# An elementwise product moved from VectorE to GpSimd, and two exponentials set apart, in a fused attention and MLP kernel

## The chip, the cores and the metric

The kernel runs on one core of a Trainium2 chip. The time is the device time of one execution in microseconds (us); before the change it is 575.52 us, the median of three runs (574.96 to 576.21). A core has five engines with a queue of instructions each, worked off in order: TensorE (PE, matrix products), VectorE (DVE), ScalarE (ACT), GpSimd (POOL) and SyncE (SP, which here issues transfers). They wait for one another through semaphores. SBUF is the working memory with 128 partitions, PSUM the memory into which TensorE writes.

## What is computed

```python
def rmsnorm(x, g):
    rms = np.sqrt(np.mean(x * x, axis=-1, keepdims=True) + 1e-06)
    return x / rms * g
# q, k, v: batch 8, 12 heads, 448 positions, 64 per head
q_n, k_n = rmsnorm(q, g_q), rmsnorm(k, g_k)
scores = q_n @ k_n.T / sqrt(64)
attn = softmax(scores) @ v                 # [8, 12, 448, 64]
x = attn.transpose(0, 2, 1, 3).reshape(8, 448, 768)
h = (x.T @ U @ V).T                        # mixing over positions, rank 32
u = x + h
out = u + relu(u @ w_ch1) @ w_ch2          # 768 -> 3072 -> 768
```

(The reference, shortened; inputs and output are float32.)

## The kernel before

The kernel works on two heads at a time. Such a pair is called a visit here, numbered p = 0 to 47, six to a batch; t = p // 2 counts groups of four heads, for which q, k and v are loaded together. The attention of batch b + 1 is woven between the matrix products of the MLP of batch b, so that TensorE always has work.

For a visit, q and k are normalised on VectorE (`scale`, which leaves out the two gain vectors), then turned so that the 64 elements of a head lie along partitions. The first 14 visits are turned by TensorE; the others by a DMA transpose. The product of both gain vectors, `gg`, one float32 per partition, is multiplied onto the turned q (`gains`), and then come the scores and the exponentials:

```python
NPE = 14
def transposes(p):
    if p < NPE:
        turn(p); keep(p, 1); keep(p, 0)        # TensorE; VectorE multiplies while it copies
    else:
        qkTs[p] = attn.tile([P, 2, S], BF16, tag="qkT", name="qkT")       # pool of 2
        nc.sync.dma_start_transpose(qkTs[p]..., qkns[p]...)

def gains(p):
    if p >= NPE:
        nc.vector.tensor_scalar(qkTs[p][:, 1], qkTs[p][:, 1], gg, None, OP.mult)   # L292

def scores(p, kcs):
    qT, kT = qkTs[p][:, 1], qkTs[p].rearrange("d s n -> d (s n)")
    for kc in kcs:
        sc = ps_s.tile([P, 2, 512], FP32, tag="s")                        # PSUM, pool of 2
        for hh in range(2):
            pp = slice(hh * D, (hh + 1) * D)
            nc.tensor.matmul(sc[:, hh, 0:S], kT[pp, kc * SP:kc * SP + P], qT[pp, :], ...)  # L300
        scs[p, kc] = sc

def expo(p, kc):                                                          # L305
    nc.scalar.activation(E_of(p)[...], scs.pop((p, kc))[...], AF.Exp, scale=float(D) ** 0.5)
```

GpSimd casts v to bf16, once per group. Before that it copies one element of the normalised q, so that the cast doesn't start before VectorE has done the normalisation:

```python
def cast_v(t):                                                            # L224
    nc.gpsimd.tensor_copy(va_of(t)[:, :, :, 0:D], vts.pop(t)...)
def yield_port(t, pr):                                                    # L573
    nc.gpsimd.tensor_copy(scratch, qkns[2 * t + pr][0:1, 1, 0, 0, 0:1])
```

GpSimd also adds one of the four outputs of a pair of blocks in the second MLP layer (L501), and in the early part of the kernel squares some inputs (L236) and issues the loads of the MLP's weights.

The first MLP layer is produced in pieces of six matmuls (L541), each evacuated with a ReLU by ScalarE (even pieces, L544) or VectorE (odd pieces, L546). The second layer (L466) has pieces of six matmuls too; it uses sums of blocks that VectorE makes (L452, L457, L482, L493), and one copy from PSUM to PSUM by ScalarE (L481).

The order of a visit is written as a list of steps with weights. `weave` puts MLP pieces in front of each step, as many as its weight is worth; a weight of 1 is about one piece. A step of weight 0 follows the one before it directly:

```python
def idle(*_):
    pass

for p in range(b * 6, b * 6 + 6):
    t, odd = divmod(p, 2)
    if NPE <= p + 1 < NP:
        add(.5, transposes, p + 1)
    add(2 if p == 6 else 1, scores, p, (0, 1))
    add(0, expo, p, 0)
    add(0, expo, p, 1)
    add(.5, idle, p)
    # ... loads, squares ...
    add(2, values, p - 1, 0)             # E @ v of the visit before, and its division
    # ... reduce ...
    if odd and more:
        add(0, scale, t + 1, 1)
        add(0, yield_port, t + 1, 1)
        add(0, cast_v, t + 1)
    add(1, scores, p, (2, 3))
    add(0, expo, p, 2)
    add(0, expo, p, 3)
    add(.5, idle, p)
    # ...
    if p + 1 < NP:
        add(0, gains, p + 1)
    # ... rsqrt ...
    add(1.5, values, p - 1, 1)
    # ...
    if not odd and more:
        add(0, scale, t + 1, 0)
        add(0, yield_port, t + 1, 0)
```

So in an odd visit GpSimd's queue holds the one-element copy and the cast; in an even one only the copy, behind the place of `gains`.

Of the kernel before, what the change touches and what calls it, by code (L numbers as in the profile page):

```python
# [13 lines left out]
OP = AluOpType  # L14
# [3 lines left out]
def kernel(  # L18
# [13 lines left out]
    nc = tc.nc  # L32
# [55 lines left out]
    gg = consts.tile([P, 1], FP32, name="gg")  # L88
# [107 lines left out]
    qks, vts, sqs, rstds, qkns, qkTs, scs, pts = {}, {}, {}, {}, {}, {}, {}, {}  # L196
# [92 lines left out]

    def gains(p):  # L290
        if p >= NPE:
            nc.vector.tensor_scalar(qkTs[p][:, 1], qkTs[p][:, 1], gg, None, OP.mult)  # L292

    def scores(p, kcs):
        qT, kT = qkTs[p][:, 1], qkTs[p].rearrange("d s n -> d (s n)")
# [282 lines left out]
    def attention(b, extra={}, later=None):  # L578

        items = []  # L580

        def add(weight, fn, *args):
            put = items if later is None or args[0] < ahead.get(fn, NP) else later
            put.append((weight, lambda: fn(*args)))

        def late_add(fn, *args):
            later.append((0, lambda: fn(*args)))

        def idle(*_):
            pass  # L590

        def sums(p, n):
            f = {12: 0, 13: 1, 14: 3, 15: 2}.get(p)
            if f is not None:
                add(0, weight_sums, f, 3 * n)

        for p in range(b * 6, b * 6 + 6):
            t, odd = divmod(p, 2)
            more, more2 = t + 1 < NT, t + 2 < NT
            if NPE <= p + 1 < NP:  # L600
                add(.5, transposes, p + 1)
            add(2 if p == 6 else 1, scores, p, (0, 1))
            add(0, expo, p, 0)
            add(0, expo, p, 1)
            add(.5, idle, p)
            if p + 1 < NPE and not odd:
                add(.5, transposes, p + 1)
            if 7 <= p <= 10:
                add(0, mix_u, 0, p - 7, (0,))
            sums(p, 0)  # L610
            lead = 1 if b == 1 else 2
            if not odd and p > 9 and t + lead < NT:
                add(0, load, t + lead, 1, (0,))
            if not odd and more:
                add(0, squares, t + 1, ALL, (1,))
            if odd and more2:
                add(0, squares, t + 2, ALL, (0,))
            if p in extra:
                add(0, *extra[p])
            if p % 6:  # L620
                add(2, values, p - 1, 0)
            elif b > 1:
                add(1, idle)
            sums(p, 1)
            if not odd and more:
                add(0, reduce, t + 1, ALL, (1,))
# [4 lines that stand above are left out]
            if odd and 6 <= t + lead < NT:  # L631
                add(0, load, t + lead, 1, (1,))
            add(1, scores, p, (2, 3))
            add(0, expo, p, 2)
            add(0, expo, p, 3)
            add(.5, idle, p)
            if p + 1 < NPE and odd:
                add(.5, transposes, p + 1)
            if 7 <= p <= 10:
                add(0, mix_u, 0, p - 7, (1,))  # L640
# [3 lines that stand above are left out]
                add(0, rsqrt, t + 1)  # L644
            sums(p, 2)
            if p % 6:
                add(1.5, values, p - 1, 1)
            elif b > 1:
                add(1, idle)
            sums(p, 3)  # L650
# [3 lines that stand above are left out]
            if odd and more2:  # L654
                add(0, reduce, t + 2, ALL, (0,))
            if odd and 6 <= t + lead < NT:
                add(0, load_v, t + lead)
            if p == 11:
                add(0, load, 7, 1, (0,))
                late_add(load, 7, 1, (1,))  # L660
                late_add(load_v, 7)
        add(2, values, b * 6 + 5, 0)
        add(2, values, b * 6 + 5, 1)
        return items
# [256 lines left out]
    with tc.manual_schedule():  # L921
        head()
        late = {7: (load_w2s, 1, 3), 8: (load_w2s, 3, 5), 9: (load_w2s, 5, 6)}
        for b in range(B):
            fill, total = mlp(b), volume(b)
            if b + 1 < B:
                later = []
                rest = [(4, lambda: (load_w2(0, 0), transposes(6), reduce(4, ALL, (0,))))] + attention(1, late, later)
                weave(fill, total * (0.72 if b in (4, 6, ) else FA[b % 2] if b else FA0), attention(b + 1) if b else rest)
                weave(fill, total * FM, mixing(b + 1))  # L930
                if b == 0:
                    weave(fill, total * FL, [(5 if w == .5 else 1, piece) for w, piece in later])
            for _ in fill:
                pass
# [30 lines left out]
```

## Time and profile before

| | |
|---|---|
| time, median of 3 | 575.52 us (574.96 to 576.21) |
| span of the profiled execution | 573.7 us |
| exponentials, L305 on ScalarE, outputs E | 184 of 915 ns, 158.2 us |
| multiplications by the gains, L292 on VectorE | 34, median 329 ns, longest 1031 ns, from 126.0 to 484.7 us |
| DMA transposes of q and k, L287 | 34, median 2.9 us from issue to landing |
| one-element copies, L573 on GpSimd | 44 of 240 ns |

How to read it: a row of a group gives the line of the kernel, the engine, the operation, output and input with their shapes, the count, then busy us and mean ns of one, then the idle time of that engine just before, with what ended it. A line of the timeline gives start, duration, engine, line and operation, and in square brackets how long the engine had idled. In the list of waits an arrow points at what ended the wait. A matmul's end is modelled, so PE's busy share is not its share of peak speed, but its idle time is time in which nothing was running on it. PEld is the loading of weights, which runs beside PE.

### The profile page before, as it was taken

Reading aid. Unit: us, or ns where it says so; the run is one execution under the profiler, and the core shown is the slowest. Engines: PE = TensorE matmul, PEld = TensorE weight load, DVE = VectorE, ACT = ScalarE, POOL = GpSimd, SP = SyncE. Lnnn points to the kernel's source line nnn. Section 1 sums busy time; section 2 is a strip of 40 time slices with the busy share of each in tenths; the row PEclk is TensorE's granted clock in tenths of the full one; section 3 lists DMA queues with packets and bytes.
Section 4 is the critical chain, followed back from the end, with each engine's and each line's share of the span. In section 5 each row is a group of like instructions: output and inputs, shape, how many; then the busy total and the mean of one; then the engine's idle time right before and its main releaser. Section 6 shows DMA issues by size and latency. Waiting matters only on the chain.

```text
span 573.7 us, 11376 instructions
## 1 busy us (share of the span) xinstructions
PE 558.7 (97%) x4640; PEld 311.0 (54%) x4661; DVE 386.7 (67%) x755; ACT 280.2 (49%) x419; POOL 78.6 (14%) x124
## 2 busy tenths in 40 slices
PE   7988999999999999999999999999999999999997
PEld 5554555544565555544565555644456555654464
DVE  5977865799875788557776588747767486443442
ACT  4966652476621875076631777146661476302200
POOL 4653600100020000000020010000011000000010
PEclk9999999999999999999999999999999999999999
DMA  8999996632644567435534456555334541140021
GB/s 202 242 237 234 213 178 150 165 91 61 129 120 111 123 118 159 92 85 114 130 87 106 106 131 141 120 118 129 87 81 122 121 98 33 30 110 2 0 56 55
DMA packets 103648, 67.22 MB, mean 117 GB/s; under 512 B 54716, under 2 KB 102060, under 8 KB 103596
## 3 DMA queue, kind: packets, MB, share of 16 engines
q1 hardware_dynamic: 93988, 56.77, 42.3%
q0 software_dynamic: 9376, 9.44, 9.9%
q8 instruction: 36, 0.59, 0.4%
q10 hardware_dynamic: 232, 0.30, 0.1%
q14 instruction: 16, 0.13, 0.1%
HBM read 52.19 MB, written 11.01 MB: 110 GB/s over the span
## 4 chain that ended last, share of the span: by engine, by line
PE 87%; DMA 7%; DVE 3%; ACT 1%; SPq 1%; issue 1%; POOL 0%; DVEq 0%
PE ph L541 37%; PE pb L466 10%; PE po L466 8%; PE pe L466 7%; PE pa L466 7%; PE bank L326 7%; PE sc L300 7%; DMA w1b<-in_moe_w_ch_dram 3%; DMA vt<-in_v_dram 2%; PE pu L379 2%; ACT E L305 1%; PE o L326 1%; DVE ring L381 1%; PE pm L365 1%; DMA qk<-in_q_dram 1%
## 5 line engine op out<-in xcount | busy, mean ns | idle before, releaser
L541 PE MATMUL ph<-u,w1b 128*128 128x384 bf16 (+1 forms) x1107 | 231.5, 353 | 3.3 <-DMA w1b<-in_moe_w_ch_dram 1.6
L305 ACT ACTIVATE E<-sc 112x896 bf16<-112x896 f32 x184 | 158.2, 915 | 55.9 <-PE sc L300 55.8
L541 PEld LDWEIGHTS <-w1b 128*128 128x128 bf16 x1128 | 102.6, 98 | 109.5 <-issue 22.6
L466 PEld LDWEIGHTS <-hT 128*128 128x128 bf16 x1080 | 101.5, 98 | 71.0 <-issue 8.4
L544 ACT ACTIVATE hT<-ph 128x384 bf16<-128x384 f32 (+1 forms) x95 | 51.6, 543 | 132.1 <-PE ph L541 128.4
L546 DVE TENSOR_SCALAR hT<-ph 128x512 bf16<-128x512 f32 (+1 forms) x93 | 57.8, 622 | 50.3 <-PE ph L541 50.3
L326 PEld LDWEIGHTS <-E 112*128 112x128 bf16 x1472 | 59.0, 98 | 14.3 <-issue 1.4
L300 PE MATMUL sc<-qkT 64*128 64x448 bf16 x384 | 54.9, 354 | 2.4 <-ACT E L305 1.9
L256 DVE TENSOR_TENSOR qkn<-qk,rstd 112x512 bf16<-112x512 f32 x84 | 54.4, 686 | 3.9 <-ACT rstd L248 2.5
L242 DVE TENSOR_REDUCE rstd<-sq 112x16 f32<-112x1024 f32 x40 | 48.4, 1211 | 12.6 <-ACT sq L234 12.6
L326 PE MATMUL bank<-va,E 112*128 112x65 bf16 x1280 | 54.1, 194 | 0.0
L573 POOL COPY scratch<-qkn 1x1 bf16<-1x1 bf16 x44 | 10.5, 240 | 307.8 <-DVE qkn L256 307.8
L466 PE MATMUL po<-w2b,hT 128*128 128x384 bf16 x288 | 52.3, 326 | 0.1
L466 PE MATMUL pa<-w2b,hT 128*128 128x384 bf16 x264 | 49.1, 326 | 0.0
L466 PE MATMUL pb<-Tw,hT 128*128 128x384 bf16 x264 | 48.5, 326 | 0.0
L234 ACT ACTIVATE sq<-qk 112x1024 f32<-112x1024 f32 x36 | 38.2, 1061 | 6.7 <-DVE rstd L242 5.2
L381 DVE TENSOR_TENSOR ring<-pu,ring 128x768 bf16<-128x768 f32 (+3 forms) x36 | 31.0, 864 | 15.0 <-PE pu L379 14.2
L501 POOL TENSOR_TENSOR o<-o,ring 128x384 f32<-128x384 f32 x11 | 12.6, 1144 | 161.6 <-DVE o L500 161.6
L343 DVE TENSOR_TENSOR ring<-bank,rec 128x192 bf16<-128x192 f32 (+1 forms) x83 | 32.3, 389 | 1.9
L336 DVE RECIPROCAL rec<-bank 128x4 f32<-128x4 f32 x83 | 14.8, 178 | 26.6 <-PE bank L326 26.2
L300 PEld LDWEIGHTS <-qkT 64*128 64x128 bf16 x384 | 12.3, 94 | 33.8 <-issue 31.1
L481 ACT ACTIVATE pb<-pa 128x384 f32<-128x384 f32 x11 | 5.3, 480 | 50.1 <-PE pa L466 50.1
(111 smaller groups left out, 450.0 us busy)
## 6 DMA issues: line engine op xcount, KB each, us to landing
qk<-in_k_dram SPq DMA_DIRECT2D x21, 448.0 KB, 5.4
vt<-in_v_dram SPq DMA_DIRECT2D x20, 448.0 KB, 4.5
qk<-in_q_dram SPq DMA_DIRECT2D x19, 448.0 KB, 3.8
w2b<-in_moe_w_ch_dram POOLq DMA_DIRECT2D x6, 768.0 KB, 15.2
w1b<-in_moe_w_ch_dram POOLq DMA_DIRECT2D x2, 1536.0 KB, 17.8
out_dram<-o SPq DMA_DIRECT2D x15, 168.0 KB, 2.7
out_dram<-o SPq DMA_DIRECT2D x16, 144.0 KB, 2.0
out_dram<-o SPq DMA_DIRECT2D x15, 120.0 KB, 2.1
```

The source lines that it names most:

```text
L234: nc.scalar.activation(sqs[t, s][:, hs], qks[t, s][:, hs], AF.Square)
L242: nc.vector.tensor_reduce(rstds[t][:, s, hs].rearrange("p h j -> p (h j)"), sqs[t, s][:, hs].rearrange("p h (j d) -> p (h j) d", d=D), AX, ...
L256: nc.vector.tensor_tensor(qkn[:, s].rearrange("p j h d -> p h j d"), qks[t, s][:, hp].rearrange("p h (j d) -> p h j d", d=D), rstd[:, s, h ...
L300: nc.tensor.matmul(sc[:, hh, 0:S], kT[pp, kc * SP:kc * SP + P], qT[pp, :], start=True, stop=True)
L305: nc.scalar.activation(E_of(p)[:, :, PAD + kc * S:PAD + (kc + 1) * S], scs.pop((p, kc))[0:SP, :, 0:S], AF.Exp, scale=float(D) ** 0.5)
L326: nc.tensor.matmul(o[:, n, :], E[:, hh, c:c + P], va[:, hl, kc, :], start=(kc == 0), stop=(kc == NJ - 1))
L343: nc.vector.tensor_tensor(ring[:, r0:r0 + t1 - t0, d0:d0 + D], o[:, t0:t1, 0:D], rec[:, t0:t1].rearrange("p c -> p c ()").to_broadcast([P, ...
L381: nc.vector.tensor_add(xv, pu[rows, 0:n, 0:HALF], xv)
L466: nc.tensor.matmul(ps, lhs[:, c, :], rhs[:, c, :], start=first and c == 0, stop=last and c == NC - 1, skip_group_check=again)
L541: nc.tensor.matmul(ph, w1b[:, dc, hc * P:(hc + 1) * P], u[:, dc, :], start=(dc == 0), stop=(dc == KD - 1))
L544: nc.scalar.activation(hT[:, hc, 0:n], ph, AF.Relu)
L546: nc.vector.tensor_relu(hT[:, hc, 0:n], ph)
```

## The change

Two things are done at once. The multiplication of the turned q by the gains, for the visits that are turned by DMA (14 to 47), goes from VectorE's queue to GpSimd's; it stands at the same place in the program. It is meant to take work off VectorE, which is busier than GpSimd. And the two exponentials of half a visit, which followed each other directly with an empty step of weight 0.5 after them, are set apart: the second has the weight 0.5 itself, so that where a piece of the MLP falls there, its evacuation comes between them. It lets that evacuation by ScalarE go ahead of the second exponential. The order of TensorE's and SyncE's instructions stays as it is.

```diff
     def gains(p):
         if p >= NPE:
-            nc.vector.tensor_scalar(qkTs[p][:, 1], qkTs[p][:, 1], gg, None, OP.mult)
+            nc.gpsimd.tensor_scalar(qkTs[p][:, 1], qkTs[p][:, 1], gg, None, OP.mult)
@@
-        def idle(*_):
+        def idle():
             pass
@@
             add(0, expo, p, 0)
-            add(0, expo, p, 1)
-            add(.5, idle, p)
+            add(.5, expo, p, 1)
@@
             add(0, expo, p, 2)
-            add(0, expo, p, 3)
-            add(.5, idle, p)
+            add(.5, expo, p, 3)
```

## The prediction

> **What bounds the kernel now.** I read the page first: busy shares, then the chain that ended last.
>
> ```profile
> PE 558.7 (97%) x4640; PEld 311.0 (54%) x4661; DVE 386.7 (67%) x755; ACT 280.2 (49%) x419; POOL 78.6 (14%) x124
> ...
> PE 87%; DMA 7%; DVE 3%; ACT 1%; SPq 1%; issue 1%; POOL 0%; DVEq 0%
> ```
>
> TensorE (PE) is busy 97% of the span and is 87% of the chain. VectorE (DVE), from which the change takes work, is 3% of it. Then busy time by stage, each row: start:end, length, then busy us of PE, weight loads, DVE, ACT, POOL. The multiplications that move lie between 126 and 485 us (the line's own listing), so these stages matter:
>
> ```profile
> 109.00:149.00 40.00, 39.63 (x294) 18.18 (x299) 35.68 (x65) 27.40 (x39) 2.79 (x6) 1.00 0.50 119
> ...
> 451.00:484.00 33.00, 32.92 (x298) 18.09 (x295) 24.20 (x55) 23.91 (x38) 2.73 (x6) 1.00 0.39 88
> ```
>
> PE idles 0.37 and 0.08 us here. The same difference over all eleven rows from 109 to 484 sums to 1.7 us, so nothing in this stretch can win more than that, a third of a percent, while PE's work is unchanged. Last, PE's waits, the first two rows (total, times, longest):
>
> ```profile
> PE bank L915 <- POOL ring L132: 3.1, 1, 3.1
> PE sc L300 <- ACT E L305: 1.9, 6, 0.4
> ```
>
> Only the second concerns the change: scores waiting for an exponential to free one of two PSUM buffers, 1.9 us in all.
>
> **What the Trainium skill says.** (1) *GPSIMD Engine Reference*, 3.1 Elementwise: an elementwise body of few operations is bound by its port at 1.03 cycles an element, the clock being 1.2 GHz (1. Specifications). That is 0.86 ns an element. The trace agrees, by its two contiguous GpSimd casts:
>
> ```profile
> L224 POOL CAST va<-vt 112x1024 bf16<-112x1024 f32 x20 | 20.7, 1033 | 1.2 <-DMA vt<-in_v_dram 1.2
> ...
> L680 POOL CAST Tw<-Tw 112x128 bf16<-112x128 f32 x1 | 0.3, 283 | 0.0
> ```
>
> (1033 - 283) / (1024 - 128) = 0.84 ns an element. (2) *SBUF — State Buffer*, "SBUF: two separate sides": VectorE and GpSimd share a port pair as an exclusive lock; whoever has it keeps it for the whole instruction, the other fully blocks. The trace agrees; I show it below (the multiplication of 0.33 us took 1.03 us beside a cast). (3) *Perfetto Trace Analysis*, "Optimizing Scalar/DVE Operations": because of that port, moving work between these two might not help. No run here shows that for this operation yet.
>
> **The change, part by part.**
>
> *A. 34 multiplications leave VectorE.* Their median is 0.329 us on DVE (line 292's listing), so DVE loses 34 x 0.33 = 11 us, and about 4 us more in the seven places where a cast blocked it (0.77 to 1.03 us instead of 0.33). DVE is not on the end's path: no gain by itself.
>
> *B. 34 multiplications come to GpSimd.* 448 bf16 elements a partition: 283 + 320 x 0.84 = 551 ns, say 0.55 us (estimate from the two casts; the scalar per partition may add some). GpSimd rises by 34 x 0.55 = 19 us to about 97. What counts is when each result is there against the scores that read it. Half of them come in even visits: GpSimd has been idle for microseconds, and the product is there as soon as the transpose has landed, where DVE made it late. The others, in odd visits, stand behind the cast of v in GpSimd's queue. There I went through all 34 in the timeline and compared the time the cast ends, plus 0.55, plus 0.14 of signalling (below), with the start of the next scores:
>
> ```profile
> 195.19 1.03 POOL L224 CAST va<-vt 112x1024 bf16<-112x1024 f32 x1
> ...
> 195.24 1.26 DVE L457 TENSOR_TENSOR hT<-hT 128x512 bf16<-128x512 bf16 x1
> ...
> 196.42 0.32 DVE L292 TENSOR_SCALAR qkT<-qkT,gg 128x448 bf16<-128x448 bf16 x1
> ...
> 196.89 0.56 PE L300 MATMUL sc<-qkT 64*128 64x448 bf16 x4
> ...
> 210.76 1.03 DVE L292 TENSOR_SCALAR qkT<-qkT,gg 128x448 bf16<-128x448 bf16 x1
> ```
>
> (Columns: start, duration, engine.) At 196 the product ends at 196.74 and the scores start 0.15 us later: they wait for it already, though no row of waits says so. DVE's sum (L457) was blocked by the cast until 196.22 and ended at 196.50. If GpSimd must then wait for that sum, its product runs 196.50 to 197.05 and the scores start at 197.19, 0.30 late. The same picture stands at 331 and 465: 3 x 0.30 = 0.9. At 210.76 a product took 1.03 us instead of 0.33, because a cast held the lock from 210.62 to 211.65. On GpSimd it starts when that cast ends, so the scores, now at 212.05, start at 211.65 + 0.55 + 0.14 = 212.34, 0.29 late. At 345, by the same sum, 0.05. All others have 0.25 us or more to spare. Loss: 1.24 us.
>
> *C. Two waits go.* At 189.7 and 458.1 the scores also start 0.14 after a product that DVE made late (behind a reduction). On GpSimd, idle then, it comes in time. The weight load before the scores at 189.7 waited 0.39 us against the usual 0.32: 2 x 0.07 = 0.14 us gained. Parts B and C: 1.24 - 0.14 = +1.1 us.
>
> *D. The second exponential after the MLP piece.* PE's order is the same, instruction for instruction; only ScalarE's changes. Of the 84 pairs of exponentials from visit 6 on, 15 come to have a ScalarE instruction between them (12 evacuations of the first MLP layer, 3 copies of the second; elsewhere the piece's evacuation is VectorE's or there is no piece). In 14 of them the next scores start 4.0 us or more later, and scores, piece, evacuation and exponential take about 0.5 + 1.3 + 0.2 + 0.5 + 0.9 = 3.4 us: no effect. The exception is visit 6:
>
> ```profile
> 47.88 0.55 PE L300 MATMUL sc<-qkT 64*128 64x448 bf16 x4
> 49.98 1.15 PE L541 MATMUL ph<-u,w1b 128*128 128x384 bf16 x6 [1.55 <-DMA w1b<-in_moe_w_ch_dram]
> ...
> 48.28 1.72 ACT L305 ACTIVATE E<-sc 112x896 bf16<-112x896 f32 x2 [1.18 <-PE sc L300]
> 51.22 0.49 ACT L544 ACTIVATE hT<-ph 128x384 bf16<-128x384 f32 x1 [1.21 <-POOL sq L236]
> ```
>
> Now both exponentials run 48.28 to 50.00, inside the time in which the MLP piece waits for its weights. After, the second stands behind the evacuation of that piece: 51.22 + 0.49 = 51.71, then 0.9, ends at 52.6. The next scores start at 51.46 as now, but their second half, which wants its buffer, would start at 51.7 and must wait until about 52.65. The next two exponentials shift too; following the chain to the scores of visit 7, which now start their second half at 53.64 after a 0.25 wait, I get 54.44. Loss: 0.8 us. In exchange an evacuation comes about 1 us earlier in 15 places, but PE waits for none of them in the table above: gain 0.
>
> *Sum.* 575.5 + 1.1 + 0.8 = 577.4; as PE has a little idle time afterwards in which a part could be swallowed, I take 577.2 us.
>
> **The rivals.** *1. VectorE is freed and that pays.* For it: its busy share at 109 to 149 is 35.68 of 40 us, and its products are late behind reductions. Against it: PE's idle time in that stretch is 0.37 us. At the best, all of A and C with no stall in B, and visit 6 swallowed: about 574.5 us.
>
> *2. GpSimd's product is slow, or the lock bites often.* If the scalar read from memory makes it 1.2 us instead of 0.55, all products after a cast lose 0.65 us of slack. Those with slack under 0.7 now (five above, and those at 126.7 and 145.4) would lose some 0.6 each, 4 us in all; and VectorE's two-input sums would be blocked 34 times. That makes 580 to 582 us. For it: L573's copy of one element stretches from 0.18 to 0.78 us beside a VectorE sum (161 us). Against it: most products have over 1 us to spare.
>
> *3. Nothing.* The stalls of B need the lock to fall to VectorE and coincide with the scores; if GpSimd goes straight from cast to product, the three cases of 0.30 become 0.02 and the sum is about +1: 576.5 us.
>
> **Range and chances.** Centre 577.2. The low end, 575.3, is no loss in B with half the loss of D; the high end, 580.0, is the second rival in part. The three runs before spread by 1.25 us. Two percent is 11.5 us: faster by that is beyond all idle time of PE after 109 us, and slower needs about 0.35 us lost at each of 34 products. Faster 0.01, same 0.96, slower 0.03.
>
> **What would show each step right or wrong.** A: DVE's busy time falls from 387 to about 372, PE's time stays. B: the new GpSimd row shows x34 at 0.5 to 0.6 us, and scores near 197, 212, 331 and 465 wait 0.2 to 0.4 us longer; right times with no longer wait would refute the lock's part. D: near 51.7 the scores show a wait for ACT of some 0.9 us, and PE's waits for exponentials grow from 1.9 to about 2.8 us. The prediction fails if the product takes over 1 us, if PE waits on GpSimd in rows that I gave slack, or if an evacuation that I called early enough proves to have held PE up.

## The result and the profile after

The changed kernel takes 582.42 us (median of 4 runs, 581.92 to 583.84) against 575.87 us (median of 4, 574.96 to 578.51): ratio 1.011, 95% interval 1.0072 to 1.0148. It is slower by 6.5 us where 1.7 was predicted, and outside the range of 575.3 to 580.0.

The lines of the page of the changed kernel that answer to those shown of before, busy shares and the chain that ended last:

```profile
PE 559.5 (96%) x4640; PEld 311.7 (54%) x4661; DVE 379.1 (65%) x721; ACT 281.7 (48%) x419; POOL 128.0 (22%) x158
...
PE 83%; DMA 6%; DVE 4%; POOL 3%; SPq 1%; issue 1%; ACT 1%; POOLq 0%; DVEq 0%; ACTq 0%
```

TensorE's busy time is the same within a microsecond; GpSimd, 0% of the chain before, is 3% of it now. TensorE's first waits in total, changed kernel (total, times, longest):

```profile
PE sc L300 <- POOL qkT L292: 5.7, 6, 1.2
PE ph L541 <- DMA w1b<-in_moe_w_ch_dram: 3.6, 1, 3.6
PE bank L913 <- POOL ring L132: 3.1, 1, 3.1
PE sc L300 <- ACT E L305: 1.9, 6, 0.4
```

The first row is new: six times the scores wait for a product on GpSimd, 5.7 us in all. The second was 1.6 us in the profile before; it is the landing of the first layer's weights at the start and varies from run to run, as the experiments show. The stretches that were shown of before, moved by the delay that the scores have there (3.1 and 7.4 us):

```profile
112.10:152.10 40.00, 37.73 (x271) 17.12 (x275) 34.29 (x59) 25.40 (x36) 8.30 (x9) 1.00 0.49 117
458.40:491.40 33.00, 32.00 (x292) 17.94 (x290) 22.66 (x50) 24.03 (x37) 9.90 (x11) 1.00 0.40 88
```

TensorE idles 2.27 us where it idled 0.37, and 1.00 where it idled 0.08. And the groups of GpSimd, which give the reason:

```profile
L292 POOL TENSOR_SCALAR qkT<-qkT,gg 128x448 bf16<-128x448 bf16 x34 | 49.9, 1467 | 82.2 <-DMA qkT<-qkn 36.4 <-PE sc L300 22.8 <-PE bank L326 11.8
L224 POOL CAST va<-vt 112x1024 bf16<-112x1024 f32 x20 | 20.7, 1034 | 1.4 <-DMA vt<-in_v_dram 1.4
```

The product of 448 elements takes 1467 ns (median 1405), longer than the cast of 1024 elements and over two and a half times the 551 ns that I had worked out.

Where the time went shows best when the start of each scores instruction is compared between the two traces. From 110 us on the difference is a staircase. It starts at 3.08 us and rises at six places, named by the time before: +1.26 at 126.7, +0.85 at 145.4, +0.95 at 196.9, +0.95 at 331.3, +0.80 at 345.5, +0.95 at 465.3. That is 5.76 us; three steps down (-0.38 at 245.7, where a wait of 0.23 us for a transfer is gone, and -0.10 each at 189.7 and 458.1) bring the end to 8.28. All six late products are made in odd visits, where they stand behind the cast. At the third of them, timeline of the changed kernel, GpSimd, VectorE and TensorE:

```profile
200.28 1.03 POOL L224 CAST va<-vt 112x1024 bf16<-112x1024 f32 x1
...
200.33 1.29 DVE L457 TENSOR_TENSOR hT<-hT 128x512 bf16<-128x512 bf16 x1
...
201.30 1.59 POOL L292 TENSOR_SCALAR qkT<-qkT,gg 128x448 bf16<-128x448 bf16 x1
...
202.94 0.56 PE L300 MATMUL sc<-qkT 64*128 64x448 bf16 x4 [1.00 <-POOL qkT L292]
```

The product runs from the end of the cast to 202.89 and the scores start 0.05 us later, after 1.00 us of idle TensorE. It took 1.59 instead of 1.40 us because VectorE's sum, blocked by the cast, came in between: the mechanism that I had named, with a product of another length.

### The profile page after: what moved, and what is told of

Read it like the earlier page. It is cut to its first block, busy times and chain, and to the rows that moved or that the text cites. A ratio compares the mean times of both kernels' runs of the same rounds, so it can differ in the third digit from the quotient of the medians.

```text
span 582.0 us, 11431 instructions
## 1 busy us (share of the span) xinstructions
PE 559.5 (96%) x4640; PEld 311.7 (54%) x4661; DVE 379.1 (65%) x721; ACT 281.7 (48%) x419; POOL 128.0 (22%) x158
## 4 chain that ended last, share of the span: by engine, by line
PE 83%; DMA 6%; DVE 4%; POOL 3%; SPq 1%; issue 1%; ACT 1%; POOLq 0%; DVEq 0%; ACTq 0%
PE ph L541 33%; PE pb L466 11%; PE po L466 8%; PE pe L466 7%; PE pa L466 7%; PE sc L300 6%; PE bank L326 6%; DMA w1b<-in_moe_w_ch_dram 4%; DMA vt<-in_v_dram 3%; PE pu L379 2%; POOL qkT L292 2%; DVE qkn L256 2%; POOL va L224 1%; PE o L326 1%; SPq L209 1%
## 5 line engine op out<-in xcount | busy, mean ns | idle before, releaser
L305 ACT ACTIVATE E<-sc 112x896 bf16<-112x896 f32 x184 | 159.8, 916 | 60.3 <-PE sc L300 60.2
L292 POOL TENSOR_SCALAR qkT<-qkT,gg 128x448 bf16<-128x448 bf16 x34 | 49.9, 1467 | 82.2 <-DMA qkT<-qkn 36.4
L256 DVE TENSOR_TENSOR qkn<-qk,rstd 112x512 bf16<-112x512 f32 x84 | 54.4, 686 | 5.2 <-ACT rstd L248 3.0
L501 POOL TENSOR_TENSOR o<-o,ring 128x384 f32<-128x384 f32 x11 | 12.6, 1148 | 151.4 <-DVE o L500 151.4
```

The lines of the kernel that those rows point to most:

```text
L256: nc.vector.tensor_tensor(qkn[:, s].rearrange("p j h d -> p h j d"), qks[t, s][:, hp].rearrange("p h (j d) -> p h j d", d=D), rstd[:, s, h ...
L292: nc.gpsimd.tensor_scalar(qkTs[p][:, 1], qkTs[p][:, 1], gg, None, OP.mult)
L305: nc.scalar.activation(E_of(p)[:, :, PAD + kc * S:PAD + (kc + 1) * S], scs.pop((p, kc))[0:SP, :, 0:S], AF.Exp, scale=float(D) ** 0.5)
```

## The experiments

The theory after the result: the product takes 1.4 us on GpSimd, and where it stands behind the cast it comes too late for six scores; the separated exponentials cost 0.5 to 0.8 us once; the rest of the 3 us before 110 us is chance. The rivals: the exponentials are the real cost; the lock between the engines slows VectorE; GpSimd is too slow wherever the product stands. All edits are against the kernel before, which ran on the same chip: median 576.56 us beside the first four, 576.77 beside the last four. (e4 and e8, which leave the gains out in part or wholly, serve for durations alone.)

**The gains alone** (e1_gains_only).

```diff
-            nc.vector.tensor_scalar(qkTs[p][:, 1], qkTs[p][:, 1], gg, None, OP.mult)
+            nc.gpsimd.tensor_scalar(qkTs[p][:, 1], qkTs[p][:, 1], gg, None, OP.mult)
```

> The gains on GpSimd, the exponentials side by side as before. Theory 1 (the product, 1.4 us on GpSimd, stands behind the cast of v and comes too late for the scores of six visits; the exponentials cost 0.5 to 0.8 us once): 5 to 6 us over the kernel before, six waits of about 1 us of the scores for GpSimd. Rival (the separated exponentials are the cost, and GpSimd's late product only takes the blame): under 1.5 us over the kernel before.

Measured: 582.14 us, ratio 1.0106 (1.0081 to 1.0132), so 5.6 us over. Its waits:

```profile
PE sc L300 <- POOL qkT L292: 5.7, 6, 1.2
...
PE ph L541 <- DMA w1b<-in_moe_w_ch_dram: 2.1, 1, 2.1
```

The staircase is the same to 0.01 us at each of the six places. This half alone makes nearly the whole loss.

**The exponentials alone** (e2_exps_only).

```diff
-            add(0, expo, p, 1)
-            add(.5, idle, p)
+            add(.5, expo, p, 1)
@@ the same for expo(p, 3)
```

> The exponentials set apart, the gains on VectorE as before. Theory 1: 0.5 to 1 us over the kernel before, all of it at visit 6, scores level from there on. Rival (separated exponentials are the cost): 4 us or more over. A third theory (the 2 us by which the first MLP weights landed later in the changed kernel's profile belong to the change of order): 2 to 3 us over and the later landing seen here too.

Measured: 575.95 us, ratio 1.0002 (0.9984 to 1.0019). From 110 us on the staircase has one step over 0.1 us, -0.26 at 245.7, the place of the transfer again. The cost at visit 6 is there all the same, timeline of this run:

```profile
50.50 0.56 PE L267 MATMUL pt<-ident,qkn 112*128 112x112 bf16 x8
...
50.74 0.49 ACT L544 ACTIVATE hT<-ph 128x384 bf16<-128x384 f32 x1 [0.52 <-PE ph L541]
...
51.13 2.53 ACT L305 ACTIVATE E<-sc 112x896 bf16<-112x896 f32 x3
...
52.09 0.36 PE L300 MATMUL sc<-qkT 64*128 64x448 bf16 x2 [0.74 <-ACT E L305]
...
57.72 0.55 PE L300 MATMUL sc<-qkT 64*128 64x448 bf16 x4
```

The same stretch before, and then the place in the changed kernel:

```profile
50.97 0.56 PE L267 MATMUL pt<-ident,qkn 112*128 112x112 bf16 x8
...
57.64 0.55 PE L300 MATMUL sc<-qkT 64*128 64x448 bf16 x4
```

```profile
53.46 0.95 PE L267 MATMUL pt<-ident,qkn 112*128 112x112 bf16 x8
...
55.10 0.37 PE L300 MATMUL sc<-qkT 64*128 64x448 bf16 x2 [0.35 <-ACT E L305]
```

The evacuation now stands between the exponentials of visit 6 and the second pair of scores waits 0.74 us. From the transposes (L267) to the second scores of visit 7 it takes 7.22 us, against 6.67 before and 6.68 with the gains alone: +0.55 us. In the changed kernel itself the same wait is only 0.35 us. Its transposes took 0.95 us instead of 0.56, in a stretch, 51.1 to 54.5 us, in which the granted clock was 0.50. Two of the runs below, e3 and e5, have such a stretch there too, and so can't be compared at this place.

The start of the kernel varies by more than this cost. e1 and, further below, e3, e5 and e7 differ from the kernel before only from the first of the moved products on, at about 122 us; yet their scores at 110 us are +1.98, +0.19, +4.07 and -0.93 us from it. Their waits for the first weights are 2.1, 2.5, 2.9 and 3.2 us, after 1.6 in the profile before; with the exponentials apart there is none in this run, 2.9 in e6 (below) and 3.6 in the changed kernel. So the third theory falls: the later landing follows neither half of the change. Of the 3.08 us in the changed kernel, 2.0 are its longer wait for the weights and 0.9 the MLP piece behind it, which took 1.90 us at the lower clock instead of 0.99. The interval of the timing, about 1 us to either side, is wider than 0.55 us, so the cost of the exponentials is shown in the traces and not in the total.

**The product in front of the cast** (e3_gains_before_cast).

```diff
-nc.vector.tensor_scalar(...)
+nc.gpsimd.tensor_scalar(...)
@@ in the list of a visit
+            if odd and p + 1 < NP:
+                add(0, gains, p + 1)
             if odd and more:
                 add(0, scale, t + 1, 1)
                 add(0, yield_port, t + 1, 1)
                 add(0, cast_v, t + 1)
@@
-            if p + 1 < NP:
+            if not odd and p + 1 < NP:
                 add(0, gains, p + 1)
```

> The gains on GpSimd, but in odd visits put in front of the one-element copy and the cast of v in its queue; the exponentials as before. Theory 1 (lateness behind the cast is all): no wait of scores for GpSimd is left, time within 0.5 us of the kernel before, although GpSimd and VectorE share as much work as with the gains alone. Rival (the lock between VectorE and GpSimd slows VectorE enough to hold up TensorE wherever the product stands): still 3 us or more over the kernel before.

Measured: 577.14 us, ratio 1.0011 (0.9995 to 1.0027); 0.6 us over by the medians, with no difference inside the interval. One wait for GpSimd is left:

```profile
PE sc L300 <- POOL qkT L292: 0.3, 1, 0.3
```

GpSimd is busy 131.9 us here, even more than in the changed kernel (128.0), and VectorE 376.5. At 196.9 the queue now reads:

```profile
194.72 1.86 POOL L292 TENSOR_SCALAR qkT<-qkT,gg 128x448 bf16<-128x448 bf16 x1 [2.83 <-DMA qkT<-qkn]
196.53 0.18 POOL L573 COPY scratch<-qkn 1x1 bf16<-1x1 bf16 x1
196.66 1.03 POOL L224 CAST va<-vt 112x1024 bf16<-112x1024 f32 x1
```

The product is done at 196.58, and the scores start at 196.89 without a wait, though the lock stretched it to 1.86 us. So with as much load and a product as slow, all six waits are gone: it is the place in the queue that makes them. The lock is not free, though. Once in this run it reaches TensorE, by way of VectorE:

```profile
296.57 2.71 DVE L452 TENSOR_TENSOR S<-hT 128x1536 bf16<-128x1536 bf16 x1
...
299.88 0.67 PE L326 MATMUL bank<-va,E 112*128 112x65 bf16 x16 [0.39 <-DVE ring L343]
```

VectorE's sum took 2.71 us after 0.94 before: it met the cast, late behind a product that the lock had stretched to 3.28 us, and a sum of GpSimd (L501) after it. TensorE waited 0.39 us. The wait for GpSimd that is left, 0.29 us, is at 338.4 (time before), for a product of an even visit. With the product in front the cast ended later (332.82, before 330.63); the next load of v, which needs the tile that the cast reads, went right after it in both runs, and the transpose behind that load in SyncE's queue started at 333.33 instead of 331.13, 2.2 us later where the scores were 0.7 us late. From 110 us to the end this trace loses 0.67 us, which fits the 0.6 of the medians. What is put in front of the cast makes the cast late in its turn.

**Five forms of the product** (e4_forms; groups of heads t modulo 5, forms 1 and 3 leave the gains out).

```diff
+            form = (p // 2) % 5
+            if form == 0:   nc.gpsimd.tensor_scalar(x, x, gg, None, OP.mult)
+            elif form == 1: nc.gpsimd.tensor_scalar(x, x, 1.0, None, OP.mult)
+            elif form == 2: nc.gpsimd.tensor_tensor(x, x, gg.to_broadcast([P, S]), OP.mult)
+            elif form == 3: nc.gpsimd.tensor_copy(x, x)
+            else:           # two halves y of 224 elements
+                nc.gpsimd.tensor_scalar(y, y, gg, None, OP.mult)
```

> The gains on GpSimd in five forms, by group of heads: as in the change; a constant 1.0 in place of the gains (leaves the gains out); a two-input product with the gains broadcast; a plain copy in place (leaves the gains out); and the change's form in two halves of 224 elements. If the scalar read from memory makes the product slow, the constant takes about 0.55 us and the change's form 1.4. If the multiplying loop itself is slow, both take 1.4 and the copy 0.55. If bf16 is slow, the copy takes 1.4 too. Two halves: 0.75 us each if most of it is per element, 1.1 each if most is per instruction.

Measured, listing of the tile's instructions on GpSimd in this run (ns: least, median, most):

```profile
L305 POOL TENSOR_SCALAR qkT<-qkT,gg x12: 832/842/1117, 165.1 to 404.3; 128x224 bf16<-128x224 bf16 x12
L299 POOL TENSOR_TENSOR qkT<-qkT,gg x8: 922/932/1298, 128.7 to 474.5; 128x448 bf16<-128x448 bf16 x8
L301 POOL COPY qkT<-qkT x8: 549/558/1078, 147.4 to 485.7; 128x448 bf16<-128x448 bf16 x8
L295 POOL TENSOR_SCALAR qkT<-qkT,gg x6: 1392/1402/1589, 199.2 to 422.6; 128x448 bf16<-128x448 bf16 x6
L297 POOL TENSOR_SCALAR qkT<-qkT x6: 1318/1322/1329, 214.4 to 460.8; 128x448 bf16<-128x448 bf16 x6
```

A copy takes 558 ns: my 551 was right for a copy. The one-scalar product takes 1402, with a constant 1322, so the scalar from memory costs only 80. From 224 to 448 elements it grows by 560 ns, 2.5 ns an element with 282 ns fixed, where the casts had given 0.84. And the product with two inputs, which reads the gains broadcast, is faster, 932 ns.

**Types and operation** (e8_types; all forms leave the gains out; `fa` is a float32 tile, `x` the turned q).

```diff
+            if form == 0:   nc.gpsimd.tensor_scalar(fa, fa, gg, None, OP.mult)
+            elif form == 1: nc.gpsimd.tensor_scalar(fa, x, gg, None, OP.mult)
+            elif form == 2: nc.gpsimd.tensor_tensor(fa, fa, gg.to_broadcast([P, S]), OP.mult)
+            elif form == 3: nc.gpsimd.tensor_copy(fa, x)
+            else:           nc.gpsimd.tensor_scalar(x, x, 1.0, None, OP.add)
```

> What sets the length of the product on GpSimd, by group of heads: float32 in and out with the scalar from memory; bf16 in and float32 out with the same; a two-input product in float32 with the gains broadcast; a copy bf16 to float32; adding a constant in bf16. All leave the gains out of the result. If bf16 input or output is what makes the one-scalar form slow, the float32 form takes about 0.55 us; if it is the form's loop, all three one-scalar forms take 1.2 to 1.4 us and the two-input product stays near 0.93.

Measured, listing of the float32 tile's instructions on GpSimd:

```profile
L300 POOL TENSOR_TENSOR fa<-fa,gg x8: 922/932/1327, 128.4 to 467.8; 128x448 f32<-128x448 f32 x8
L302 POOL CAST fa<-qkT x8: 549/558/1082, 146.9 to 482.8; 128x448 f32<-128x448 bf16 x8
L296 POOL TENSOR_SCALAR fa<-fa,gg x6: 1397/1402/1598, 199.2 to 415.8; 128x448 f32<-128x448 f32 x6
L298 POOL TENSOR_SCALAR fa<-qkT,gg x6: 1392/1402/1567, 213.3 to 458.2; 128x448 f32<-128x448 bf16 x6
```

and of the turned q:

```profile
L304 POOL TENSOR_SCALAR qkT<-qkT x6: 1327/1330/1495, 164.6 to 401.8; 128x448 bf16<-128x448 bf16 x6
```

Types change nothing (1402 in float32 and in mixed types too, 932 for two inputs, 558 for a cast), and the addition of a constant takes 1330, about as long as the product with one. The length belongs to the one-scalar form of the instruction. Why GpSimd runs it slower than the two-input form, these runs don't tell.

**The shorter form behind the cast** (e5_two_input).

```diff
-nc.vector.tensor_scalar(...)
+nc.gpsimd.tensor_tensor(qkTs[p][:, 1], qkTs[p][:, 1], gg.to_broadcast([P, S]), OP.mult)
```

> The gains on GpSimd behind the cast, as in the change, but as a two-input product with the gains broadcast (0.93 us in the run of the forms, 0.47 less than 1.40); exponentials as before. Theory (each of the six waits is the product's lateness, so it shrinks one for one with the product): waits of about 0.7, 0.3, 0.5, 0.5, 0.3 and 0.5 us, 2.8 to 3.0 in sum, so about 3 us over the kernel before. Rival (the waits come from the order of the queue or a slow signal from GpSimd, not from the product's length): six waits of about 1 us as before, 5.5 us over.

Measured: 579.66 us, ratio 1.0055 (1.0034 to 1.0075), 2.9 us over, as expected in the total, but partly by luck. The waits fell further than expected, to five in the list, four of about 0.3 us and one of 0.25:

```profile
PE sc L300 <- POOL qkT L292: 1.5, 5, 0.3
```

Its six steps are +0.19, +0.37, +0.27, +0.27, +0.31 and +0.26, 1.67 us, where I had expected 2.8 to 3.0. The timeline of this run at the same place as above shows why at three of them:

```profile
199.86 1.03 POOL L224 CAST va<-vt 112x1024 bf16<-112x1024 f32 x1
...
199.91 2.16 DVE L457 TENSOR_TENSOR hT<-hT 128x512 bf16<-128x512 bf16 x1
...
200.86 0.92 POOL L292 TENSOR_TENSOR qkT<-qkT,gg 128x448 bf16<-128x448 bf16 x1
...
201.84 0.56 PE L300 MATMUL sc<-qkT 64*128 64x448 bf16 x4 [0.31 <-POOL qkT L292]
```

Here GpSimd went straight on and VectorE's sum stayed blocked through both instructions (2.16 us); with the one-scalar form VectorE's sum came first. The product was 0.67 us shorter (0.92 after 1.59), and the wait fell from 1.00 to 0.31. So the wait follows the time at which the product ends, nearly one for one. The trace from 110 us on accounts for 1.8 us of this run's loss; the timing says 2.0 to 4.3. What lies between I put down to the start, where this profile has 4.07 us of delay at 110 us with a wait of 2.9 us for the weights; that is argued, not shown.

**Only even visits on GpSimd** (e7_split).

```diff
+            if p % 2:
+                nc.gpsimd.tensor_scalar(qkTs[p][:, 1], qkTs[p][:, 1], gg, None, OP.mult)
+            else:
                 nc.vector.tensor_scalar(qkTs[p][:, 1], qkTs[p][:, 1], gg, None, OP.mult)
```

(The product for an odd p is made in the even visit before.)

> Only the 17 products of even visits, with nothing ahead of them in GpSimd's queue, go to GpSimd in the change's form of 1.4 us; those of odd visits stay on VectorE; exponentials as before. Theory (only standing behind the cast hurts): no wait of scores for GpSimd, time within 0.5 us of before, perhaps 0.2 under, for two waits behind a reduction go. Rival (1.4 us on GpSimd is too slow anywhere, by itself or by the lock): 2 us or more over.

Measured: 576.36 us, ratio 1.0003 (0.9986 to 1.0019). TensorE has no wait for GpSimd, though the 17 products are as slow as ever:

```profile
L293 POOL TENSOR_SCALAR qkT<-qkT,gg x17: 1404/1405/1448, 130.5 to 479.8; 128x448 bf16<-128x448 bf16 x17
```

The two waits behind a reduction go: steps of -0.10 at 189.7 and at 458.1, too small to be seen in the time.

**Both halves, mended** (e6_both_mended): the exponentials set apart, the product in front of the cast and in the two-input form (the edits of e2, e3 and e5 together).

> Both parts of the change, with the product in front of the cast in odd visits and as the two-input form. Theory: no wait of scores for GpSimd of more than 0.1 us, time within 0.5 us of the kernel before; VectorE's 15 us less buy nothing. Rival (VectorE's relief pays once the lateness is gone): 1 us or more under the kernel before.

Measured: 576.95 us, ratio 1.0007 (0.9987 to 1.0027): the same as before. None of TensorE's listed waits is for the product. The cost at visit 6 shows again: 7.21 us from the transposes to the second scores of visit 7. As a test of VectorE's relief this run is weak, for VectorE is hardly relieved: it is busy 384.5 us, only 2.2 less than before, because its normalisations (L256) now take 62.5 us after 54.4 beside the earlier products. The better test is e3, with 10.2 us less on VectorE (376.5), and e7 with 5.6 less (381.1): neither is faster. So the rival falls, and none of these versions beats the kernel before.

## Why the prediction was wrong

**The step that failed is the size of one product in B**: "283 + 320 x 0.84 = 551 ns, say 0.55 us (estimate from the two casts; the scalar per partition may add some)". It is 1405 ns, and six scores waited 5.7 us for it behind the cast where I had 1.24. I took a cast's time per element for a product's. The Trainium skill's figure (*GPSIMD Engine Reference*, 3.1 Elementwise: 1.03 cycles an element for bodies of few operations, clock 1.2 GHz) fits the copies and casts of this case (558 and 1033 ns for 448 and 1024 elements, 0.82 ns an element) and seemed to confirm the step; the one-scalar product measures 2.5 ns an element, about 3 of those cycles, so for it the measurement decides against the page's figure. Nothing in the trace before held the one-scalar form on GpSimd, and I should have given its length a wide range of its own. But the trace did hold products there, the squares of the inputs, which I passed over (listing of GpSimd before):

```profile
L236 POOL TENSOR_TENSOR w2b<-hT 112x1024 f32<-112x1024 f32 x4 | 7.5, 1886 | 6.1 <-DMA hT<-in_k_dram 3.4 <-DMA hT<-in_q_dram 2.7
...
L236 POOL TENSOR_TENSOR w2b<-qk 112x512 f32<-112x512 f32 x2 | 2.1, 1034 | 0.8 <-DMA qk<-in_k_dram 0.8
```

They grow by (1886 - 1034) / 512 = 1.66 ns an element, twice the cast's 0.84, which gives 1034 - 64 x 1.66 = 928 ns for 448 elements (an estimate from these two rows). That is what the two-input form then took (932), and it would have said that a cast is no measure for a product.

**With 1.40 the same sum comes near, in part by luck.** The cast's end plus 1.40 plus 0.14, against the scores: 0.60 at 126.7, 0.44 at 145.4, 0.90 at 345.5, and 0.28 of VectorE's sum besides at 196.9, 331.3 and 465.3, 1.15 each: 5.4 us. The trace has 5.76 at the same six places, but less at the last four (the scores start 0.05 us after a product on GpSimd, not 0.14) and more at the first two, where the lock stretched the product. The sum also gives 1.14 at a seventh place, which isn't there (below). Only two of the six (126.7 and 145.4) were ones to which I had given slack; rival 2 named these two, and it named 580 to 582 us at a product of 1.2. I gave that rival too small a part of the range.

**The lock's part in B** was right in kind: 1.59 instead of 1.40 us at 201. At 126.7 and 145.4 it was dearer than I had it: the product took 2.15 and 1.90 us, at 126.7 beside two sums of VectorE, which is why the steps there are 1.26 and 0.85 and not 0.60 and 0.44.

**One place of B was wrong in the other direction.** At 212 I expected 0.29 late, and with 1.40 it would be 1.14; no wait is there. The scores came 6.04 us later than before (218.09 after 212.05) but the cast only 4.84 (215.46 after 210.62): VectorE no longer stood 1.80 us behind a transpose at 204 with the product in its queue, so the cast was released that much earlier. e7, where this one product stays on VectorE and the one before it goes to GpSimd, agrees: it has 1.47 us to spare there, after 0.26 before. Taking a product out of VectorE's queue does bring something, at one place in 34.

**A**: DVE's time fell by 7.6 us, not 15. The products are gone (14.9 us), but VectorE's sums wait longer at the lock: the four of 1536 elements (L452) take 6.6 us in all after 3.8. That TensorE's work stayed was right, and so was that VectorE's relief is worth nothing: e3 has 10.2 us of it without the six waits and gains nothing.

**C** was right: -0.10 us at each of the two places, where I had 0.07.

**D** was right in place and kind, and somewhat too large: 0.55 us in e2 and e6 for 0.8. The second pair of scores starts 0.90 us later in e2 against the first pair, where I had 0.95; but the wait of 0.25 us at visit 7, which I had kept, goes. The sign that I had named for D, PE's waits for exponentials growing from 1.9 to 2.8 us, fails in the changed kernel: they stay at 1.9, because in its slower stretch at visit 6 the wait is only 0.35 (e2 has 2.3). That the other 14 separations are free, and that the earlier evacuations bring nothing, e2 bears out.

## What to carry to other kernels

Before moving an operation to another engine, measure that very form there: here a copy took 558 ns and a product 932 or 1402, the two-input form being the faster. Then ask what stands ahead of it in the new queue and how long before its reader it can start: here 17 slow products with nothing ahead of them cost nothing, all 34, with none behind the cast, 0.6 us by the medians (with no difference inside the interval), and 34 with half of them behind the cast 5.6. Ask too what then stands behind it: the cast put back delayed a load and with it a transpose. An engine with 14% busy time is not free at the moment that counts, and 10 us of relief for VectorE, which TensorE hardly waited for, were worth nothing.

## What the runs showed of the hardware

On GpSimd, 448 elements a partition: copy or cast 558 ns, two-input product with one side broadcast 932, one-scalar product or sum 1322 to 1402; the product with the gains took 1402 in bf16, in float32 and from one to the other. And when VectorE waits at the lock while GpSimd has a second instruction behind the first, either may come next: VectorE's sum got in before a one-scalar product (1.29 us for the sum), but stayed out behind a two-input one (2.16 us), at the same three places.
